# Block-sparse attention and a token mix on one core: V of a head pair kept in SBUF, value products in 32x32 tiles

## The chip, the cores and the metric

The kernel runs on one core of a Trainium2 chip. The metric is the device time of one execution in microseconds; before the change three runs took 635.79, 639.23 and 639.93 us, a median of 639.23. A profiled execution is a run of its own, and all rows of the profile below come from that one.

The engines are named as the profile names them: PE is the matrix engine (PEld its weight loads), DVE the vector engine, ACT the scalar engine, POOL the general-purpose engine and SP the engine that issues most of the DMAs.

## The reference

Attention over 4 batches, 8 heads, 768 tokens and a head size of 64, masked by blocks of 32 tokens. A query block sees its own and both neighbouring key blocks, the first and the last block, and three blocks that an input table names for it; the first and the last query block see everything. The result, heads side by side, goes through a token mix.

```python
scores = scale * np.matmul(q, k.transpose(0, 1, 3, 2))
mask = np.abs(blk_i - blk_j) <= window
mask = mask | (blk_i == 0) | (blk_j == 0) | (blk_i == n_blocks - 1) | (blk_j == n_blocks - 1)
for qb in range(n_blocks):
    for kb in sampled_blocks[qb]:
        mask[qb * block:(qb + 1) * block, kb * block:(kb + 1) * block] = True
attn = np.exp(scores)
attn = attn / (np.sum(attn, axis=-1, keepdims=True) + 1e-09)
...
theta = x @ w_theta
cos_t, sin_t = (np.cos(theta), np.sin(theta))
yr = np.einsum('ts,bsd->btd', w_tok_r, x * cos_t)
yi = np.einsum('ts,bsd->btd', w_tok_i, x * sin_t)
u = x + yr + yi
return u + np.maximum(u @ w_ch, 0.0)
```

The weights arrive as 64-bit floats. The kernel decodes them on the chip, piece by piece, into a high part of reduced precision and a low part that holds the rest; the token mix multiplies with both.

## The kernel before

A "pair" is two of the four batches, with all their heads: 16 heads, of which `b` numbers the batch (2), `e` a half of the heads (2) and `p` four heads of 32 columns each. The program does attention for both pairs and writes the result to a DRAM tile `xs`, then the token mix, which reads it back.

Attention works through 60 units. Of each pair, 8 are edge units (`"w"`: one batch, one half of the heads, the first or the last query block against all 24 key blocks) and 22 are inner units: one query block for all 16 heads against 8 key blocks. A unit passes through five stages: `scores` (PE, f32, tiles of 64 rows by 32 columns, so eight run side by side), a minimum over the negated scores (DVE), `weights` (ACT: exponentials), `turn` (PE: eight 128x128 transposes; ACT copies them out of PSUM) and `values` (PE: 128 rows, 32 columns, 65 moving columns of V and a column of ones), and `finish` (DVE divides by the sum; SP writes `xs`).

The eight key blocks of an inner unit stand in `kg`: ACT copies the neighbours and ends (line 235), DVE the three sampled blocks by numbers held in registers (line 244). Their values come straight from DRAM, row by row: the window blocks into `va` (line 263, a ring of three blocks, two tiles), the sampled blocks into `vb` by an indirect DMA from POOL (line 270, three tiles). The edge units' V comes in tiles `vw` of its own.

The order of the attention stage is written out by hand under `manual_schedule` (lines 403 to 445): in turn n, DVE finishes unit n-2, ACT and DVE gather keys for n+2, PE does the scores of n+1, the transposes of n and the values of n-1. So on PE the runs stand scores, transposes, values, in a steady round of 56 matmuls per inner unit as the program writes them. The decoding of the weights is spread over the turns in thirds of a piece (`Decoder.ahead` on ACT, `go` on DVE, 22 pieces). K of a pair lies in one tile `kb`; the second pair's K is loaded over it from the ACT queue when the first pair is nearly done.

The token mix has no hand-written order. Its matmuls run in f32r with high and low parts, 48 steps of theta (lines 517 to 519), mix (555 to 557) and an output product (578 to 580).

Of the kernel before, what the change touches and what calls it, by code (L numbers as in the profile page):

```python
# [10 lines left out]
F32 = mybir.dt.float32  # L11
# [8 lines left out]
P = 128  # L20
NB = 24
NP = 2
ZEROS = float(768 * NP)
VB_BUFS = 3
Q_AHEAD = 4
# [20 lines left out]
class Piece:  # L46
# [5 lines left out]
    def __init__(self, nc, hi, lo, src, name):  # L52
        self.nc, self.hi, self.lo, self.src, self.name = nc, hi, lo, src, name
        self.f = src.shape[1] // 2
# [10 lines left out]
    def bits(self):  # L65
        nc, a, ai = self.nc, self.a, self.a.bitcast(I32)
        nc.vector.tensor_scalar(a, a, WORD_LO, WORD_HI, op0=ALU.max, op1=ALU.min)
        nc.vector.tensor_scalar(ai, ai, 4, 1, op0=ALU.logical_shift_left, op1=ALU.logical_shift_right)
        nc.vector.scalar_tensor_tensor(ai, self.raw[:, :, 1], SIGN_BIT, ai, op0=ALU.bitwise_and, op1=ALU.bitwise_or)
# [12 lines left out]
    def low(self):  # L82
        self.nc.vector.tensor_tensor(self.a, self.a, self.hi.bitcast(F32), op=ALU.subtract)
        self.nc.vector.tensor_tensor(self.lo, self.a, self.raw[:, :, 0].bitcast(F32), op=ALU.add)


class Decoder:


    def __init__(self, pieces, pool, queue):  # L90
        self.pieces, self.pool, self.queue = pieces, pool, queue
        self.at = 0
        for piece in pieces[:2]:
            piece.load(pool, queue)

    def left(self):
        return max(3 * len(self.pieces) - self.at, 0)

    def ahead(self, n):

        for k in range(self.at, min(self.at + n, 3 * len(self.pieces))):
            piece = self.pieces[k // 3]
            if k % 3 == 0:
                piece.start()
            elif k % 3 == 2:
                piece.high()

    def go(self, n):
        for k in range(self.at, min(self.at + n, 3 * len(self.pieces))):
            piece = self.pieces[k // 3]  # L110
            (piece.bits, piece.rest, piece.low)[k % 3]()
            if k % 3 == 2 and k // 3 + 2 < len(self.pieces):
                self.pieces[k // 3 + 2].load(self.pool, self.queue)
        self.at += n


class Tables:


    def __init__(self, nc, cp, sampled):  # L120
        self.raw = cp.tile([P, NB * 6], I32, name="sb_raw")
        nc.sync.dma_start(self.raw, sampled.rearrange("i k -> (i k)").partition_broadcast(P))

    def make(self, nc, cp):
        raw = self.raw
        words = raw.rearrange("p (i k w) -> p i k w", k=3, w=2)
        given = cp.tile([P, 3, NB], F32, name="sb_given")
        nc.vector.tensor_copy(given, words[:, :, :, 0].rearrange("p i k -> p k i"))
        r = cp.tile([P, 3, NB], F32, name="sb_r")
        nc.vector.tensor_scalar(r, given, 0.0, float(NB - 1), op0=ALU.max, op1=ALU.min)  # L130
        self.block = cp.tile([1, NB * 3], I32, name="sb_block")
        nc.vector.tensor_copy(self.block.rearrange("p (i k) -> p k i", k=3), r[0:1])
        iota_i = cp.tile([P, NB], I32, name="iota_i")
        nc.gpsimd.iota(iota_i, pattern=[[1, NB]], base=0, channel_multiplier=0)
        qi = cp.tile([P, NB], F32, name="qi")
        nc.gpsimd.tensor_copy(qi, iota_i)
        first_i = cp.tile([96, NP], I32, name="first_i")
        for k in range(3):
            nc.gpsimd.iota(first_i[32 * k : 32 * k + 32], pattern=[[768, NP]], base=0, channel_multiplier=1)
        first = cp.tile([96, NP], F32, name="first_row")  # L140
        nc.gpsimd.tensor_copy(first, first_i)
# [3 lines left out]
        nc.vector.tensor_tensor(t, r, qi.unsqueeze(1).to_broadcast([P, 3, NB]), op=ALU.subtract)  # L145
# [9 lines left out]
        self.rows = rows = cp.tile([96, NP, NB], I32, name="rows")  # L155
        for k in range(3):
            g = slice(32 * k, 32 * k + 32)
            nc.vector.tensor_scalar(t[g, 0, :], u[g, k, :], -1.0, 1.0, op0=ALU.mult, op1=ALU.add)
            for bp in range(NP):
                nc.vector.tensor_scalar(t[g, 1 + bp, :], r[g, k, :], 32.0, first[g, bp : bp + 1], op0=ALU.mult, op1=ALU.add)  # L160
        left, base = t[0:96, 0:1, :], t[0:96, 1:3, :]
        nc.vector.scalar_tensor_tensor(base, base, -ZEROS, left.to_broadcast([96, NP, NB]), op0=ALU.add, op1=ALU.mult)
        nc.vector.tensor_scalar(rows, base, ZEROS, None, op0=ALU.add)


def attention(tc, qT, qE, kT, vr, sampled, xs, ident, pieces, follow):
# [9 lines left out]
    with ExitStack() as ctx, ExitStack() as early:  # L176
# [3 lines left out]
        ps_s = early.enter_context(tc.tile_pool(name="ps_s", bufs=2, space=PSUM, side="right"))  # L180
        gp = ctx.enter_context(tc.tile_pool(name="gp", bufs=1))
        vp = ctx.enter_context(tc.tile_pool(name="vp", bufs=2))
# [4 lines left out]
        ps_t = ctx.enter_context(tc.tile_pool(name="ps_t", bufs=1, space=PSUM))  # L187
        ps_x = ctx.enter_context(tc.tile_pool(name="ps_x", bufs=2, space=PSUM))
# [5 lines left out]
        kgs = [gp.tile([P, 8, 8, 32], F32, name=f"kg{x}") for x in range(2)]  # L194
        vas = [cp.tile([P, 1040], F32, name=f"va{x}") for x in range(2)]
        vbs = [cp.tile([P, 1040], F32, name=f"vb{x}") for x in range(VB_BUFS)]
        kbs, qbs, qes, vws, st, xws, numbers = {}, {}, {}, {}, {}, {}, {}
# [8 lines left out]
        def load_k(bp, b, p0=0, n=4, queue=nc.sync):  # L206
            if (b, p0) == (0, 0):
                kbs[bp] = kp.tile([P, 8, NB, 32], F32, tag="kb", name=f"kb{bp}")
            queue.dma_start(kbs[bp][:, 4 * b + p0 : 4 * b + p0 + n], kT[bp, b][:, p0 : p0 + n])

        def load_edges(bp):
            raw = ep.tile([P, 512], F32, tag="qw", name=f"qw{bp}")
            nc.sync.dma_start(raw, qE[bp])
            qes[bp] = raw

        def turn_edges(bp):
            t = ep.tile([P, 2, 2, 4, 32], F32, tag="qe", name=f"qe{bp}")
            nc.vector.tensor_scalar(t.rearrange("r z b p f -> r (z b p f)"), qes[bp], -0.125, None, op0=ALU.mult)
            qes[bp] = t
# [3 lines left out]
        def number_blocks(bp, i):  # L223
            _, numbers[bp, i] = nc.values_load_multi_w_load_instructions(
                tab.block[0:1, 3 * i : 3 * i + 3], engines=[mybir.EngineType.DVE], min_val=0, max_val=NB - 1,
                skip_runtime_bounds_check_because="Tables clamps the block numbers",
            )

        def gather_k(bp, i):
            kg, kb = kgs[i % 2], kbs[bp]  # L230
            def blocks(b0, n):
                return kb[:, :, b0 : b0 + n, :].rearrange("r g s f -> r s g f")

            def copy(s0, b0, n):
                nc.scalar.activation(kg[:, s0 : s0 + n], blocks(b0, n), AF.Copy, scale=-0.125)

            if i <= 2:
                copy(3, 0, 1)
                copy(7, NB - 1, 1)
            for b0, n in fresh(i, i <= 2):  # L240
                copy(b0 % 3, b0, n)
# [473 lines left out]
```

## Time and profile before

| | |
|---|---|
| Median of three runs | 639.23 us |
| The profiled execution | 636.82 us |
| Its span, first to last instruction | 635.0 us |
| Mean granted clock of PE | 0.964 |
| Busy in the span: PE, DVE, ACT, POOL | 563.2, 463.5, 361.0, 45.6 us |
| First matmul; first theta matmul | 8.45 us; 286.74 us |
| Moved by DMA | 96.52 MB, 152 GB/s over the span |

A group of instructions is shown with its line, engine and operation, what it writes and reads, the count, its busy time, the mean duration in ns, and after the second bar the idle time of the engine just ahead of it with what ended that. A wait is shown as who waited for whom, us in total, times, and the longest. "issue" as a releaser means that the engine waited for nothing that the profile shows. Busy time of PE is not PE at its peak, since matmuls overlap and their ends are modelled.

### The profile page before, as it was taken

The numbers are of one execution on the slowest core, as the hardware profiler recorded it, in microseconds if no ns is written. First come the engines' busy times: TensorE is split into PE (matmuls) and PEld (weight loads), VectorE is DVE, ScalarE is ACT, GpSimd is POOL, SyncE is SP. The second block draws the span as 40 slices with busy tenths as digits, with TensorE's granted clock in tenths as the row PEclk, the third lists the DMA queues.
The fourth block names the chain that finished last, engine by engine and source line by source line (L and its number), as shares of the span: only waits on it lengthen the run. The fifth ranks groups of instructions, "written<-read, shape, count | busy, mean of one in ns | idle before, by whom it ended". The sixth has DMA issues, their size and how long they took to land.

```text
span 635.0 us, 19148 instructions
## 1 busy us (share of the span) xinstructions
PE 563.2 (89%) x7808; PEld 483.1 (76%) x7808; DVE 463.5 (73%) x1239; ACT 361.0 (57%) x774; POOL 45.6 (7%) x56
## 2 busy tenths in 40 slices
PE   4987778769887768668999999999999999999997
PEld 1555545545455546547999999999999999999997
DVE  1897978875798878758999697575973767746554
ACT  1586768764587767656667564355642465524520
POOL 0101212211002211110000000000000000000000
PEclk9998989988898999887999999999999999999999
DMA  8859979999778997866542224211241211211002
GB/s 287 259 156 246 275 209 259 258 278 345 219 204 244 251 257 226 221 161 170 139 130 73 64 84 143 69 47 50 80 124 59 70 51 42 80 59 61 27 1 99
DMA packets 79959, 96.52 MB, mean 152 GB/s; under 512 B 5312, under 2 KB 64832, under 8 KB 79488
## 3 DMA queue, kind: packets, MB, share of 16 engines
q1 hardware_dynamic: 73088, 72.99, 39.2%
q0 software_dynamic: 4928, 17.57, 10.7%
q10 hardware_dynamic: 1856, 4.74, 2.1%
q8 instruction: 61, 1.00, 0.7%
q14 instruction: 26, 0.21, 0.1%
HBM read 82.70 MB, written 12.58 MB: 150 GB/s over the span
## 4 chain that ended last, share of the span: by engine, by line
PE 66%; DMA 18%; DVE 8%; issue 4%; ACT 2%; SPq 1%; DVEq 1%; ACTq 0%
PE y L555 10%; PE y L556 10%; PE y L557 10%; DMA va<-in_vr_dram 10%; PE X L318 4%; PE S L288 4%; PE T L307 4%; PE h L519 3%; PE h L518 3%; PE o L578 3%; PE h L517 3%; PE o L580 3%; PE o L579 3%; DMA kb<-in_kT_dram 3%; PE SW L357 2%
## 5 line engine op out<-in xcount | busy, mean ns | idle before, releaser
L300 ACT ACTIVATE P<-S,m 128x256 f32<-128x256 f32 x176 | 69.0, 477 | 15.1 <-DVE m L291 14.9
L307 PEld LDWEIGHTS T<-ident,P 128*128 128x128 f32 x352 | 42.1, 150 | 38.2 <-ACT P L300 25.9
L307 PE MATMUL T<-ident,P 128*128 128x128 f32 x352 | 60.5, 304 | 11.2 <-ACT P L300 6.1
L318 PE MATMUL X<-va,pT 128*32 128x65 f32 (+1 forms) x1408 | 50.3, 233 | 21.9 <-DMA va<-in_vr_dram 18.1
L291 DVE TENSOR_REDUCE m<-S 128x2 f32<-128x512 f32 x88 | 56.7, 686 | 16.7 <-PE S L288 9.8
L309 ACT COPY pT<-T 128x1024 f32<-128x1024 f32 x44 | 44.8, 1018 | 41.5 <-PE T L307 41.4
L288 PE MATMUL S<-kg,q 64*32 64x256 f32 x1408 | 55.1, 404 | 10.9 <-issue 10.9
L555 PE MATMUL y<-w_tok_r_hi,zh 128*128 128x384 f32 x192 | 64.6, 336 | 0.0
L556 PE MATMUL y<-w_tok_r_lo,zh 128*128 128x384 f32 x192 | 64.4, 335 | 0.0
L557 PE MATMUL y<-w_tok_r_hi,zl 128*128 128x384 f32 x192 | 64.3, 335 | 0.0
L556 PE MATMUL y<-w_tok_i_lo,zh 128*128 128x384 f32 x192 | 64.2, 334 | 0.0
L555 PE MATMUL y<-w_tok_i_hi,zh 128*128 128x384 f32 x192 | 64.2, 334 | 0.0
L557 PE MATMUL y<-w_tok_i_hi,zl 128*128 128x384 f32 x192 | 62.7, 334 | 0.0
L270 POOL DMA_INDIRECT vb<-in_vr_dram,rows x44 | 44.1, 1002 | 229.3 <-PE X L318 206.0
L318 PEld LDWEIGHTS X<-va,pT 128*32 128x32 f32 (+1 forms) x1408 | 35.6, 116 | 31.8 <-DMA va<-in_vr_dram 17.8
L517 PE MATMUL h<-w_theta_hi,xTh 128*128 128x256 f32 x192 | 55.8, 290 | 1.9 <-ACT xTh L508 1.9
L519 PE MATMUL h<-w_theta_hi,xTl 128*128 128x256 f32 x192 | 55.6, 290 | 0.5 <-DVE xTl L509 0.5
L518 PE MATMUL h<-w_theta_lo,xTh 128*128 128x256 f32 x192 | 55.3, 288 | 0.0
L318 PE MATMUL X<-vb,pT 128*32 128x65 f32 (+1 forms) x1408 | 49.8, 232 | 5.0 <-issue 5.0
L521 ACT ACTIVATE t<-h,up_int 128x256 f32<-128x256 f32 x48 | 22.7, 473 | 42.7 <-PE h L519 42.0
L528 ACT ACTIVATE cs<-rr 128x256 f32<-128x256 f32 x48 | 20.0, 416 | 45.8 <-DVE rr L526 45.8
L578 PE MATMUL o<-uh,w_ch_hi 128*128 128x384 f32 x128 | 42.5, 336 | 0.9 <-DVE of L584 0.9
(125 smaller groups left out, 1337.2 us busy)
## 6 DMA issues: line engine op xcount, KB each, us to landing
xa<-xs SPq DMA_DIRECT2D x192, 64.0 KB
va<-in_vr_dram SPq DMA_DIRECT2D x30, 260.0 KB
xr<-xs SPq DMA_DIRECT2D x24, 256.0 KB
out_dram<-of SPq DMA_DIRECT2D x32, 192.0 KB
q<-in_qT_dram SPq DMA_DIRECT2D x22, 256.0 KB
xs<-xo SPq DMA_DIRECT2D x44, 128.0 KB
vw<-in_vr_dram SPq DMA_DIRECT2D x6, 780.0 KB
raw_tok_r<-in_w_tok_r_dram SPq DMA_DIRECT2D x9, 512.0 KB
```

The lines of the kernel that those rows point to most:

```text
L288: nc.tensor.matmul(sc[32 * p : 32 * p + 32, e, b, :], q[rows, b, p, :], kg[rows, :, 4 * b + p, :], start=True, stop=True)
L291: nc.vector.tensor_reduce(m[:, e], sc[:, e], axis=AX.X, op=ALU.min)
L300: nc.scalar.activation(pt[:, e, b, :], sc[:, e, b, :], AF.Exp, bias=m[:, e, b : b + 1], scale=-1.0)
L307: nc.tensor.transpose(t[:, k, :], pt, ident)
L318: nc.tensor.matmul(x[32 * p : 32 * p + 32, g, :], pt[0:rows, k, 32 * p : 32 * p + 32], v[0:rows, v0 + 65 * p : v0 + 65 * p + 65], start=st ...
L517: nc.tensor.matmul(ps, hi[:, c, :], wh[:, c, :], start=c == 0, stop=False)
L518: nc.tensor.matmul(ps, hi[:, c, :], wl[:, c, :], start=False, stop=False)
L519: nc.tensor.matmul(ps, lo[:, c, :], wh[:, c, :], start=False, stop=c == 3)
L555: nc.tensor.matmul(acc, zh[:, dd], wh[:, j, tt], start=j == 0 and m == 0, stop=False)
L556: nc.tensor.matmul(acc, zh[:, dd], wl[:, j, tt], start=False, stop=False)
L557: nc.tensor.matmul(acc, zl[:, dd], wh[:, j, tt], start=False, stop=j == 5 and m == 1)
L578: nc.tensor.matmul(ps, wh[:, c, :], uh, start=c == 0, stop=False)
```

## The change

K and V of a pair lie in SBUF whole. There are two places, `kv0` for the first pair (it later takes the token weights' second part) and tiles of their own for the second. V is laid out by groups of 32 rows, (batch, half of the heads) to a group of partitions and a key block to 260 columns, and loaded in six pieces of 8 blocks, K and V in turn, on SP's queue.

Inner units read the three neighbouring blocks where they lie. The sampled blocks are copied on the chip: two key blocks by DVE and one by ACT into `kg` (now five blocks), three value blocks by POOL into `vg`, each engine with block numbers in registers of its own. A block that is masked or doubled is replaced by a block of zeros in V.

The value product is cut by row group: for each of eight key blocks, 4 x 2 matmuls of 32 rows, 32 columns and 65 moving columns for each batch `b`. The two batches go in two runs, with the scores and transposes of other units between them, and the second run waits for the first reduction of those scores. `X` covers two banks and has one buffer; the transposes' PSUM tile is split into two of one bank.

Edge units are cut by key blocks, not by heads: (z, t), z the first or last query block and t a third of the key blocks, six of a pair, each with all heads and 8 blocks, the same shape as an inner unit. Each third has its own maximum; POOL scales the three sums by the exponentials of the differences and adds them.

Decoding of weights: 20 pieces, theta and half of tok_r with the first pair, the rest with the second; DVE does two parts of a piece, the low part goes to POOL in two halves. w_ch is decoded in eight steps of the token mix, a whole piece each. The scale by 0.125 moves from the copies into the exponential.

Cut to its core:

```diff
-        ps_t = ctx.enter_context(tc.tile_pool(name="ps_t", bufs=1, space=PSUM))
-        ps_x = ctx.enter_context(tc.tile_pool(name="ps_x", bufs=2, space=PSUM))
+        ps_t = ctx.enter_context(tc.tile_pool(name="ps_t", bufs=2, space=PSUM))
+        ps_x = ctx.enter_context(tc.tile_pool(name="ps_x", bufs=1, space=PSUM))
...
-            for k, number in enumerate(numbers.pop((bp, i))):
-                src = kb[:, :, bass.ds(number, 1), :].rearrange("r g s f -> r s g f")
-                nc.vector.tensor_scalar(kg[:, 4 + k : 5 + k], src, -0.125, None, op0=ALU.mult)
...
-                nc.sync.dma_start(va[s0 : s0 + 32 * n], vr[768 * bp + 32 * b0 : 768 * bp + 32 * (b0 + n)])
...
-            nc.gpsimd.indirect_dma_start(
-                out=vb[0:96],
...
+            for k in range(2):
+                nc.vector.tensor_copy(kg[:, 1 + k : 2 + k], block(bp, numbers[bp, i][0][k]))
...
+            nc.scalar.copy(kg[:, 3:4], block(bp, numbers[bp, i][0][2]))
...
+            for k in range(3):
+                nc.gpsimd.tensor_copy(vg[:, k : k + 1], vs[bp][:, bass.ds(numbers[bp, i][1][k], 1)])
...
+                q, runs = qes[bp][:, z], [(0, ks[bp][:, 8 * t : 8 * t + 8])]
+            else:
+                q, runs = qbs.pop((bp, i)), [(0, ks[bp][:, i - 1 : i + 2]), (3, kgs[i % 2])]
...
-            for p in range(4):
-                nc.tensor.matmul(
-                    x[32 * p : 32 * p + 32, g, :], pt[0:rows, k, 32 * p : 32 * p + 32], v[0:rows, v0 + 65 * p : v0 + 65 * p + 65],
-                    start=start, stop=stop,
-                )
...
+            for k in used:
                 for p in range(4):
                     for e in range(2):
+                        rows = slice(32 * (2 * b + e), 32 * (2 * b + e) + 32)
+                        mm = nc.tensor.matmul(
+                            s["X"][32 * p : 32 * p + 32, e, 65 * b : 65 * b + 65], s["T"][rows, k, 32 * p : 32 * p + 32],
+                            blocks[k][rows, 65 * p : 65 * p + 65], start=k == used[0], stop=k == used[-1],
+                        )
...
+                do(n - 1, values, 0)
+                do(n + 1, scores)
+                between = st[units[n + 1]]["reduced"] if n + 1 < len(units) else None
+                do(n, turn)
...
+                do(n - 1, values, 1, between)
+                do(n, evict)
+                do(n + 1, weights)
+                do(n - 1, finish)
```

The order on PE, inner units of the first pair, before: the scores of unit 4, the transposes of 3, the values of 2. `S`, `T`, `X` are the PSUM tiles of the three stages with the unit's number, `pT` the transposed weights; a row ends with the shape and the count.

```order
L288 MATMUL S_4_842<-kg_116,q_3_141 32x256 x16
L307 MATMUL T_3_862<-ident,P_3_778 128x128 x8
L318 MATMUL X_2_882<-va_118,pT_2_776 32x65 x4
L318 MATMUL X_2_882<-vb_122,pT_2_776 32x65 x4
L318 MATMUL X_2_882<-va_118,pT_2_776 32x65 x4
L318 MATMUL X_2_882<-vb_122,pT_2_776 32x65 x4
L318 MATMUL X_2_882<-va_118,pT_2_776 32x65 x4
L318 MATMUL X_2_882<-vb_122,pT_2_776 32x65 x4
L318 MATMUL X_2_882<-va_118,pT_2_776 32x65 x4
L318 MATMUL X_2_882<-vb_122,pT_2_776 32x65 x4
```

One round is 56 matmuls. The same place on PE after the change, where `kv` is the first pair's place and `vg` the copied blocks:

```order
L284 MATMUL S_4_1691<-kv_122,q_3_769 32x96 x8
L284 MATMUL S_4_1691<-kg_113,q_3_769 32x160 x8
L284 MATMUL S_4_1691<-kv_122,q_3_769 32x96 x8
L284 MATMUL S_4_1691<-kg_113,q_3_769 32x160 x8
L326 MATMUL T_3_0_1729<-ident,P_3_1579 128x128 x4
L326 MATMUL T_3_1_1730<-ident,P_3_1579 128x128 x4
L355 MATMUL X_2_1626<-kv_122,pT_2_1576 32x65 x32
L355 MATMUL X_2_1626<-vg_115,pT_2_1576 32x65 x24
L355 MATMUL X_2_1626<-kv_122,pT_2_1576 32x65 x8
L355 MATMUL X_3_1843<-kv_122,pT_3_1803 32x65 x32
L355 MATMUL X_3_1843<-vg_116,pT_3_1803 32x65 x24
L355 MATMUL X_3_1843<-kv_122,pT_3_1803 32x65 x8
```

A round is 168 matmuls now, and the last half of one unit's values stands right ahead of the first half of the next unit's, which writes the same `X`. An edge unit on PE before (`SW`, `Tw` and `XW` are its tiles):

```order
L357 MATMUL SW_011_271<-kb_131,qe_129 32x512 x4
L357 MATMUL SW_011_271<-kb_131,qe_129 32x256 x4
L307 MATMUL Tw_010_282<-ident,PW_010_242 128x128 x6
L318 MATMUL XW_0_244<-vw_0_0_134,pTw_001_240 32x65 x24
L357 MATMUL SW_100_323<-kb_131,qe_129 32x512 x4
```

and after:

```order
L284 MATMUL S_w_273<-kv_122,qe_120 32x256 x16
L326 MATMUL T_w_0_294<-ident,P_w_201 128x128 x4
L326 MATMUL T_w_1_295<-ident,P_w_201 128x128 x4
L355 MATMUL X_w_208<-kv_122,pT_w_198 32x65 x64
L355 MATMUL X_w_406<-kv_122,pT_w_368 32x65 x64
```

There were 38 matmuls to an edge unit and 16 such units; there are 152 to one and 12 units.

On DVE, inner units, before: the division of unit 4 and after it the three copies of sampled keys.

```order
L325 TENSOR_SCALAR sm_4_1104<-X_4_1069 128x4
L326 RECIPROCAL sm_4_1104<-sm_4_1104 128x4
L328 TENSOR_TENSOR xo_4_1107<-X_4_1069,sm_4_1104 128x256
L244 ISA
L244 TENSOR_SCALAR kg_116<-kb_131 128x256
```

and after, the reduction of unit 4, the division of unit 2 and two copies:

```order
L295 TENSOR_REDUCE m_4_1724<-S_4_1691 128x2 x2
L298 TENSOR_SCALAR nm_4_1727<-m_4_1724 128x4
L368 TENSOR_SCALAR sm_2_1811<-X_2_1626 128x4
L369 RECIPROCAL sm_2_1811<-sm_2_1811 128x4
L371 TENSOR_TENSOR xo_2_1814<-X_2_1626,sm_2_1811 128x256
L234 TENSOR_LOAD sb_keys
```

The division now stands right behind the reduction of the scores two units on; it is what frees `X`.

More of the change, by code (lines that the diff above doesn't have):

```diff
@@ L602, in token_mix @@
         stage = late.enter_context(tc.tile_pool(name="stage2", bufs=1))
[L603 removed]
+        ch = ch_pieces()
+        for piece in ch[:2]:
+            piece.load(stage, nc.sync)
         for k in range(2, RAW_AHEAD):
@@ L664, in sparse_attention_then_token_mix, with first_place, second, tok @@
-    early = pieces("theta", 512) + [x for pair in zip(pieces("tok_r", 512), pieces("tok_i", 512)) for x in pair]
-    attention(tc, qT, qE, kT, vr, sampled.bitcast(I32), xs, ident, early, follow)
+    def first_place(shape, dtype, name):
+        return const.tile(shape, dtype, tag="place", name=name)
+    rest = []
+    def second():
+        if not rest:
+            rest.append(first_place([P, 2, 9 * 768], F32R, "w_second"))
+        return rest[0]
+    def tok(at):
+        tile_, k = (first, at) if at < 3 else (second(), at - 3)
+        return [tile_[:, x, 768 * k : 768 * k + 768] for x in range(2)]
```

532 lines of the change are left out of this document (273 added, 259 removed).

## The prediction

> **What bounds the kernel now.** I read the table by stage first, then the groups of instructions, then the waits, and last the timeline at the places where TensorE waits for nothing that a semaphore shows. The stage table (time, each engine's busy time and count, granted clock, DMA share, GB/s) cuts the execution at the first matmul and at the first theta matmul of the token mix:
>
> ```profile
> core 0: us, PE busy (x) PEld busy (x) DVE busy (x) ACT busy (x) POOL busy (x), PEclk, DMA share, GB/s
> 8.44:286.74 278.30, 221.84 (x5632) 143.48 (x5632) 217.51 (x559) 188.24 (x363) 44.09 (x44) 0.94 0.86 243
> 286.74:635.00 348.26, 341.38 (x2180) 339.64 (x2176) 245.42 (x675) 171.23 (x410) 0.00 (x0) 0.99 0.26 78
> ```
>
> Attention takes 278.3 us with the DMA engines at 0.86 and no compute engine full; the token mix takes 348.3 us with PE full. So attention is where the change can act, and its obvious limits are the transfers of V. The groups and waits say more:
>
> ```profile
> q8 instruction: 61, 1.00, 0.7%
> ...
> L318 PE MATMUL X<-va,pT 128*32 128x65 f32 (+1 forms) x1408 | 50.3, 233 | 21.9 <-DMA va<-in_vr_dram 18.1
> L288 PE MATMUL S<-kg,q 64*32 64x256 f32 x1408 | 55.1, 404 | 10.9 <-issue 10.9
> ...
> PE X L318 <- DMA va<-in_vr_dram: 18.1, 14, 3.5
> PEld SW L357 <- issue: 25.2, 40, 8.4
> PEld X L318 <- issue: 18.3, 42, 2.3
> PEld S L288 <- issue: 16.0, 18, 4.5
> PE S L288 <- issue: 10.9, 5, 4.0
> ```
>
> TensorE waits for "issue" about as long as for the tile `va`. What that is: the page counts 7808 matmuls and 7808 weight loads, 15,616 instructions, and queue q8 carried 61 packets and 1.00 MB: 16 KB each, so 256 instructions of TensorE in each packet. Call that a page of code. The timeline shows stops in the middle of a run of equal matmuls, where no semaphore can be at fault:
>
> ```profile
> 88.05 1.09 PE L288 MATMUL S<-kg,q 64*32 64x256 f32 x11 [3.75 <-issue]
> 98.98 0.26 PE L318 MATMUL X<-vb,pT 128*32 128x65 f32 x3 [0.59 <-issue]
> 103.62 0.26 PE L318 MATMUL X<-va,pT 128*32 128x65 f32 x4 [0.97 <-issue]
> 237.66 1.08 PE L288 MATMUL S<-kg,q 64*32 64x256 f32 x8 [4.02 <-issue]
> ```
>
> Cut at such stops, every stretch holds one page (127 matmuls, 127 loads, a wait or two):
>
> ```profile
> 98.98:103.62 4.64, 3.67 (x127) 2.77 (x127) 4.27 (x13) 4.06 (x9) 1.09 (x1) 1.00 0.76 233
> 103.62:109.33 5.71, 4.16 (x127) 2.71 (x126) 5.29 (x16) 4.43 (x11) 1.96 (x2) 1.00 1.06 285
> 109.33:115.14 5.81, 4.15 (x126) 2.73 (x127) 4.50 (x14) 4.57 (x10) 1.22 (x2) 1.00 1.03 274
> 115.14:121.96 6.82, 5.39 (x127) 3.52 (x126) 5.78 (x15) 4.44 (x9) 1.26 (x1) 1.00 0.99 278
> 121.96:125.90 3.94, 3.72 (x126) 2.76 (x127) 3.18 (x10) 3.08 (x8) 0.91 (x1) 1.00 0.80 204
> 125.90:130.10 4.20, 3.72 (x127) 2.76 (x127) 3.88 (x12) 3.80 (x8) 1.21 (x1) 1.00 0.78 203
> 225.59:229.16 3.57, 3.56 (x126) 2.68 (x127) 2.70 (x9) 2.45 (x5) 0.91 (x1) 1.00 0.74 185
> ```
>
> Six pages in a row ended in a stop, 3.94 to 6.82 us each (mean 5.2); the last row is a page without a stop behind it. The stop of 3.75 us at 88.05 fits one late packet, which the DMA view of 85.30 to 86.60 us holds:
>
> ```profile
> q8 instruction: 1, 0.02, 5.7%
> ```
>
> 5.7% of 16 engines over 1.30 us is 1.19 us of transfer; TensorE went on at 88.05, some 1.5 us after the window. I read from this that TensorE holds the page it runs and one ahead, that the next is asked for when a page is entered, and that asking, transfer and arrival take 3.6 us or more, longer the busier the DMA engines. Before, that is nearly hidden: a unit issues 208 instructions.
>
> **The change part by part.** Value matmuls: 32 per inner unit become 128 (32 rows each, 65 columns), scores 16 become 32 (96 and 160 columns), eight transposes stay. The profile counts each value and score matmul twice (L288: 1408 records, 16 issued in each of 44 units) and each record has its weight load. Inner unit before: (32+8+64) x 2 = 208 instructions; after (64+8+256) x 2 = 656, and 592 in the four units with seven blocks. Edge units: 16 of (16+6+48) x 2 = 140 before; 12 of (32+8+256) x 2 = 592 after. Attention in all: 44 x 208 + 16 x 140 = 11,392, or 44.5 pages, against 40 x 656 + 16 x 592 = 35,712, or 139.5 pages.
>
> Price of a page. Above, 3.57 us without a stop bounds it from above at a DMA share of 0.74; with stops, 3.94, 4.20 and 4.64 us at 0.76 to 0.80, and 5.71 to 6.82 at 0.99 to 1.06. After the change attention moves about 39 MB (K and V once 12.7, q 6.3, xs 6.3, weights 11.5, code 2.3); over some 550 us that is 71 GB/s, as in the token mix now (78 GB/s, share 0.26). Lower end 3.4 us: 3.57 less a little for a packet that isn't held up. Upper end 4.6. I take 3.9, in the middle of 3.57, 3.94 and 4.20.
>
> A page takes longer to come than to run: it holds one half of a unit's values (about 1.05 us, below) or scores, transposes and a few values (about 2.5 us). So a step of 656 instructions takes 656/256 x 3.9 = 10.0 us, and what else the change does lies inside it. `X` has one buffer now, so the values of a unit wait for the division of the one before: about 1.0 us, inside. The transfers of V by row, the indirect gathers and the edge tiles go: attention moves 39 MB where it moved 67.6 (243 GB/s over 278.3 us), and the waits on `va` go with them; late next is the code. Key copies (DVE two, ACT one), value copies and the weights' low parts on POOL, a second copy out of PSUM on ACT: DVE and ACT had 217.5 and 188.2 us in 60 units, 3.6 and 3.1 per unit, so some 4 of 10 us. The merged edge maxima: under 2 us on POOL, twice per pair. All of these cost nothing as long as the step is 10 us; without that cover they are the first rival. Decoding w_ch in eight steps rather than twelve: the same work on DVE, taken as 0, with 3 us either way.
>
> Start: the first third of K with the edge queries is 1.3 MB, the first matmul stays at 8.4 us; 3 us until the pages that lie ready are used up (139.5 less 1.5). In the first 30 us 7.6 MB of K, V and weights are in flight: eight pages at 5.2 instead of 3.9, 10 us more. Sum: 8.4 + 3 + 138 x 3.9 (538) + 10 + 348.3 + 1.8 outside the span (636.82 against 635.0) = 910 us. The runs' median, 639.23, is 0.4% over the profiled 636.82; I leave that out.
>
> The rule that speaks against this sum: the Trainium skill, Runtime: NRT & Kernel Launch, Instruction fetch mechanics, gives TensorE room for 2048 instructions and calls the fetch hidden, and a sentence later says two lines of 16 KiB, read in order. By the first, three steps of code would lie ready and the sum would be the first rival's; by the second it is mine. The stops at every 256 instructions above agree with two lines.
>
> **The rivals.**
>
> *The code comes in time.* Then TensorE and the single `X` set the step. Rows for it, a score run, a transpose run, a value run and the division's three instructions:
>
> ```profile
> 99.68 1.09 PE L288 MATMUL S<-kg,q 64*32 64x256 f32 x32
> 100.70 1.09 PE L307 MATMUL T<-ident,P 128*128 128x128 f32 x8
> 101.73 0.32 PE L318 MATMUL X<-va,pT 128*32 128x65 f32 x8
> ...
> 228.11 0.32 PE L318 MATMUL X<-va,pT 128*32 128x65 f32 x8
> 229.15 1.09 PE L288 MATMUL S<-kg,q 64*32 64x256 f32 x32
> ...
> L325 DVE TENSOR_SCALAR sm<-X 128x4 f32<-128x4 f32 x44 | 6.8, 156 | 12.7 <-PE X L318 12.4
> L326 DVE RECIPROCAL sm<-sm 128x4 f32<-128x4 f32 x44 | 7.8, 178 | 1.4
> L328 DVE TENSOR_TENSOR xo<-X,sm 128x256 f32<-128x256 f32 x44 | 18.7, 424 | 3.0 <-DMA xs<-xo 1.6
> ```
>
> Scores 1.02, transposes 1.03, 64 value records on four tiles 1.04 us. After, the two halves run apart, 128 records on eight tiles each: 1.04 twice if the tiles fill. With 0.76 us of division and its semaphores (1.0), a step is 5.2 us: 8.4 + 56 x 5.2 + 348.3 + 1.8 = 650 us. If no record starts sooner than now (1.04/64 = 16 ns), values take 4.2, the step 7.2, the time 762. For it: the token mix never stops for code. Against it: seven rows above. The Trainium skill, TensorE: Matmul & The Clock Gate, puts the floor between starts at about 25 ns; the trace's 16 ns lies under it, so it gets no chance of its own; by 25 ns the estimate would be 8.4 + 56 x 9.5 + 350 = 890.
>
> *Faster.* The same, with the division hidden and 4.1 us a step: 8.4 + 56 x 4.1 + 350 = 588 us. It decides where a step falls under (637 - 358.5)/56 = 5.0 us, a page under 1.9 us; the trace has none under 3.5.
>
> *The clock falls as well.* After an idle stretch TensorE runs at half speed:
>
> ```profile
> 282.50 2.42 PE L307 MATMUL T<-ident,P 128*128 128x128 f32 x8 [4.78 <-ACT P L300]
> ```
>
> 2.42 us for what took 1.09. Idle stretches would be under 3 us here, against 4.78, so I don't expect it; if it held throughout, the page with scores and transposes would run 4.9 us: 56 more, 966 us. Pages as slow as before (5.2) give 1090.
>
> **How the numbers follow.** Forecast (pages at 3.4 to 4.6 us) 0.78; slow clock or slow pages 0.10; code in time 0.08; faster 0.04. Predicted 910 us. Range: 138 x 3.4 + 372 = 840 to 138 x 4.55 + 372 = 1000, which leaves out the two rivals with code in time and the worst of the slow pages, 2 in 10. About 1% is what a measurement here can tell from no change: faster 0.04, within 1% 0.03 (the first rival's low edge), slower 0.93.
>
> **What would show it.** Right: q8 with about 176 packets (45,184 instructions) where it had 61; stretches of 256 instructions with a stop behind each, near 3.9 us; "issue" at the head of TensorE's waits with some 300 us; a DMA share near 0.25 in attention; token mix near 348 us. Wrong: steps of 5 to 7 us with waits on DVE before X, or several pages fetched at once. The step most at risk is the price of a page when the DMA engines are quiet, which no stretch of attention now shows.

## The result, and the profile after

The changed kernel takes 958.1 us (median of four runs, 950.9 to 959.59) where the kernel before takes 639.42 in the same comparison: a ratio of 1.498, 95% interval 1.490 to 1.506. The profiled execution is the run of 950.9 us, with a span of 949.1 us and a mean granted clock of 0.744 (0.964 before). One run of those below is left out, the second of the kernel with half the value matmuls and two buffers for X (783.3 us): it lies over 1.5% above the other run of its kernel.

The stage table of the changed kernel, with the columns of the prediction's first fence, cut at 8.44 us as before and at 600.60 us, a microsecond short of the end of attention's matmuls (the first matmul starts at 6.40 us now, and the first 24 theta matmuls run between the last values, from 580.50 us on):

```profile
8.44:600.60 592.16, 446.82 (x17783) 348.37 (x17769) 227.23 (x569) 192.60 (x438) 135.12 (x232) 0.60 0.20 65
600.60:948.50 347.90, 337.94 (x2156) 336.75 (x2155) 239.71 (x655) 164.78 (x396) 0.00 (x0) 0.98 0.25 75
```

The token mix is where it was: 347.9 us. All the loss lies in attention, 592.2 us for 278.3. The transfers did go: the DMA share there fell from 0.86 to 0.20. DVE, ACT and POOL are busy for 227, 193 and 135 of the 592 us. PE is busy for 447, and its clock is 0.60 of full speed. The page shows the clock in 40 slices, the instruction queue and the chain:

```profile
PEclk7655565655666675555755565699999999999999
...
q8 instruction: 156, 2.56, 1.1%
...
PE 72%; issue 12%; DVE 7%; DMA 4%; ACT 4%; SPq 0%; POOL 0%; POOLq 0%; ACTq 0%; DVEq 0%
```

156 packets of code where there were 61. The clock drops as attention starts and returns when it ends. PE's waits, matmuls first and weight loads behind them, show no DMA of V any more; "issue" and the single `X` stand in its place:

```profile
PE X L355 <- DVE xo L371: 34.8, 32, 3.1
PE X L355 <- issue: 34.0, 41, 2.1
PE S L284 <- issue: 29.0, 21, 2.3
PE X_w L355 <- issue: 16.9, 13, 3.0
...
PEld X L355 <- issue: 54.4, 60, 3.3
PEld S L284 <- issue: 42.3, 63, 2.9
PEld T L326 <- issue: 28.9, 47, 3.2
```

No stop of PE in these rows is longer than 3.3 us. The timeline shows again stops inside runs of equal matmuls (the bracket is the idle time ahead of a row):

```profile
487.58 0.57 PE L355 MATMUL X<-vg,pT 32*32 32x65 f32 x23 [0.25 <-issue]
...
493.25 0.71 PE L355 MATMUL X<-v,pT 32*32 32x65 f32 x50 [1.19 <-issue]
...
496.96 1.09 PE L355 MATMUL X<-v,pT 32*32 32x65 f32 x53 [0.84 <-issue]
...
500.63 0.38 PE L284 MATMUL S<-k,q 64*32 64x96 f32 x4 [1.22 <-issue]
...
502.49 1.97 PE L326 MATMUL T<-ident,P 128*128 128x128 f32 x8
```

The table of the stretches between those stops, columns as above:

```profile
487.58:493.25 5.67, 4.47 (x127) 3.39 (x128) 2.63 (x5) 2.46 (x6) 0.00 (x0) 0.69 0.47 153
493.25:496.96 3.71, 1.85 (x129) 1.47 (x128) 1.86 (x7) 1.68 (x5) 1.21 (x4) 0.68 0.12 40
496.96:500.63 3.67, 2.45 (x128) 1.94 (x129) 0.53 (x1) 0.00 (x0) 1.98 (x2) 0.50 0.02 4
```

Each holds one page of 256 instructions. With the DMA engines at 0.02 it takes 3.67 us, of which PE is busy for 2.45; at 0.12, 3.71 with PE busy for half. The page of 5.67 us ran while a 256 KB transfer of q went by: its code came late. The trace ties the stops to the packets: of the 65 stops on "issue" of over 0.5 us in attention, nine in ten end 1.2 to 1.6 us after the latest packet of q8 landed, while the packets come some 4 us apart. That the transposes of 502.49 took 1.97 us where 1.09 is the full-clock time shows the third thing, the lowered clock.

### The profile page after: what moved, and what is told of

Read it like the earlier page. It is cut to its first block, busy times and chain, and to the rows that moved or that the text cites. A ratio compares the mean times of both kernels' runs of the same rounds, so it can differ in the third digit from the quotient of the medians.

```text
span 949.1 us, 43861 instructions
## 1 busy us (share of the span) xinstructions
PE 786.8 (83%) x19968; PEld 686.4 (72%) x19968; DVE 467.1 (49%) x1229; ACT 358.9 (38%) x836; POOL 136.6 (14%) x242
## 4 chain that ended last, share of the span: by engine, by line
PE 72%; issue 12%; DVE 7%; DMA 4%; ACT 4%; SPq 0%; POOL 0%; POOLq 0%; ACTq 0%; DVEq 0%
PE X L355 16%; PE S L284 10%; PE T L326 8%; PE y L579 6%; PE y L581 6%; PE y L580 6%; PE X_w L355 5%; PE S_w L284 3%; PE T_w L326 2%; PE o L602 2%; PE o L603 2%; PE o L604 2%; PE h L543 2%; PE h L542 2%; PE h L541 2%
## 5 line engine op out<-in xcount | busy, mean ns | idle before, releaser
L355 PE MATMUL X<-v,pT 32*32 32x65 f32 x3456 | 74.0, 279 | 35.3 <-DVE xo L371 15.4
L355 PE MATMUL X<-kv,pT 32*32 32x65 f32 x3456 | 72.0, 274 | 37.3 <-DVE xo L371 19.5
L579 PE MATMUL y<-w_second,zh 128*128 128x384 f32 x288 | 97.3, 338 | 2.4 <-ACT zh L566 2.4
L580 PE MATMUL y<-w_second,zh 128*128 128x384 f32 x288 | 97.3, 338 | 0.0
L581 PE MATMUL y<-w_second,zl 128*128 128x384 f32 x288 | 93.3, 338 | 0.0
L355 PE MATMUL X<-vg,pT 32*32 32x65 f32 x4224 | 85.2, 280 | 8.5 <-issue 7.6
L284 PE MATMUL S<-kg,q 64*32 64x160 f32 x1408 | 77.4, 470 | 14.2 <-issue 14.2
L355 PEld LDWEIGHTS X<-vg,pT 32*32 32x32 f32 x4224 | 66.4, 127 | 11.6 <-issue 10.5
L314 ACT ACTIVATE P<-S,nm 128x256 f32<-128x256 f32 x176 | 69.2, 484 | 0.0
L579 PEld LDWEIGHTS y<-w_second,zh 128*128 128x128 f32 x288 | 54.8, 190 | 2.6 <-ACT zh L566 2.6
L580 PEld LDWEIGHTS y<-w_second,zh 128*128 128x128 f32 x288 | 54.9, 191 | 0.0
L581 PEld LDWEIGHTS y<-w_second,zl 128*128 128x128 f32 x288 | 54.5, 191 | 0.0
```

The source lines that it names most:

```text
L284: nc.tensor.matmul(sc[32 * p : 32 * p + 32, e, b, 32 * s0 : 32 * (s0 + n)], q[rows, b, p, :], keys[rows, :, 4 * b + p, :], start=True, sto ...
L314: nc.scalar.activation(pt[:, :, 2 * b + e], sc[:, e, b].rearrange("r (s f) -> r s f", s=8), AF.Exp, bias=nm[:, 2 * e + b : 2 * e + b + 1], ...
L355: mm = nc.tensor.matmul(s["X"][32 * p : 32 * p + 32, e, 65 * b : 65 * b + 65], s["T"][rows, k, 32 * p : 32 * p + 32], blocks[k][rows, 65 * ...
L579: nc.tensor.matmul(acc, zh[:, dd], wh[:, tt], start=j == 0 and m == 0, stop=False)
L580: nc.tensor.matmul(acc, zh[:, dd], wl[:, tt], start=False, stop=False)
L581: nc.tensor.matmul(acc, zl[:, dd], wh[:, tt], start=False, stop=j == 5 and m == 1)
```

## The experiments

Three theories. A: PE waits for its code, and a page costs some 3.6 to 4.2 us whatever it holds. B: array time, at the lowered clock and with the single `X`, sets the step, and code comes beside it. C: the clock, and what lowers it. The text calls the changed kernel "after". Times are medians, of two runs for those of one round and of four for those of three rounds, against 958.1 for after and the kernel before's own median of the same comparison (635.5 to 641.5).

### A page of code more, before and after

Each of the 44 inner units gets 64 matmuls of one column ahead of its scores, into the place that the scores overwrite. In the kernel before:

```diff
             sc = ps_s.tile([P, 2, 2, 256], F32, tag="S", name=f"S{bp}_{i}")
+            for _ in range(8):
+                for p in range(4):
+                    for e in range(2):
+                        rows = slice(64 * e, 64 * e + 64)
+                        nc.tensor.matmul(sc[32 * p : 32 * p + 32, e, 0, 0:1], q[rows, 0, p, :], kg[rows, 0, 0, 0:1], start=True, stop=True)
```

> The kernel before, with 64 matmuls of one column (256 TensorE instructions, one page of code) added to each of the 44 inner units; their results are overwritten by the scores. Theory A (TensorE waits for the arrival of its code): a unit goes from 208 to 464 instructions, 0.81 to 1.81 pages; at 3.9 to 5.2 us a page that is 7.1 to 9.4 us where a unit now takes 4.8, so +100 to +205 us, 740 to 845. Theory B (array time sets the step, code is hidden): 128 records of one column at no more than 16 ns are 1.0 to 2.0 us a unit, partly beside other waits: +0 to +88 us, 640 to 728. Theory C on the clock: if stops for code are what lowers the granted clock, attention falls from 0.94 to under 0.8 here, with matmuls of 128 rows as before; if it is the 32-row value tiles, it stays over 0.9.

Measured: 811.5 us, +169.9 over the 641.5 beside it (ratio 1.266, 1.256 to 1.275), or 3.86 us for each added page, with what the lowered clock below adds.

The same in the changed kernel, with K's own tile in `kg`'s place.

> The changed kernel with the same 64 matmuls of one column (one page of code) in each of the 44 inner units. Theory A (code): 44 pages more at 3.6 to 4.2 us, +158 to +185 us, 1115 to 1145. Theory B (array time at the lowered clock, with X's single buffer and DVE): 128 records of one column, at most 2 us at half clock and partly in waits, +0 to +88 us, 958 to 1046.

Measured: 1121.3 us, +163.2, or 3.71 us a page (ratio to before 1.749, 1.729 to 1.768). Both lie in A's range and far outside B's. The groups of this kernel show what the added matmuls did, busy time and mean duration, and behind the second bar the idle time ahead of them:

```profile
L283 PE MATMUL S<-kv,q 64*32 64x1 f32 x2816 | 34.3, 195 | 55.7 <-issue 55.7
L283 PE MATMUL S<-k,q 64*32 64x1 f32 x2816 | 34.2, 195 | 52.3 <-issue 52.3
```

68.5 us of array time in 44 units, and 108.0 us of waiting for nothing but "issue". The kernel before, whose value tiles have 128 rows, lost its clock with the added page. Its stage table with the page and without it:

```profile
20.00:459.00 439.00, 338.84 (x11282) 245.56 (x11274) 222.08 (x564) 187.62 (x365) 40.72 (x44) 0.75 0.54 150
...
20.00:286.74 266.74, 210.29 (x5578) 139.81 (x5577) 212.66 (x541) 185.74 (x360) 44.09 (x44) 0.93 0.85 237
```

Stops for code came in, and so did matmuls that use little of the array; which of them lowers the clock, this run doesn't tell.

### Fewer score matmuls over the same columns

ACT copies the three window blocks into `kg` too, and the scores become 16 matmuls of 256 columns again.

```diff
+            nc.scalar.copy(kg[:, 0:3], ks[bp][:, i - 1 : i + 2].rearrange("r s g f -> r s (g f)"))
...
-                q, runs = qbs.pop((bp, i)), [(0, ks[bp][:, i - 1 : i + 2]), (3, kgs[i % 2])]
+                q, runs = qbs.pop((bp, i)), [(0, kgs[i % 2])]
```

> The changed kernel with the three window blocks of K copied into the key tile by ScalarE, so that a unit's scores are 16 matmuls of 256 columns where they were 32 of 96 and 160: the same columns, 64 instructions less in each of 44 inner units; the weights' tile has one buffer, to make room. Theory A (code): 2816 instructions are 11 pages less, at 3.6 to 4.2 us: -40 to -46 us, 910 to 920. Theory B (array time): the columns are the same, so 0, or a few us more for ScalarE's copy: 955 to 975.

Measured: 911.7 us, -46.4, or 4.2 us for each of 11 pages (ratio to before 1.422, 1.413 to 1.431). The columns are the same, and ACT does more than before. A again, though the clock rose a little as well (0.65 in attention for 0.60), and its part in the 46 us isn't known.

### The same in the other direction, in the kernel before

Only the split of the scores into 96 and 160 columns is taken over from the change.

```diff
-                        nc.tensor.matmul(sc[32 * p : 32 * p + 32, e, b, :], q[rows, b, p, :], kg[rows, :, 4 * b + p, :], start=True, stop=True)
+                        for s0, s1 in ((0, 3), (3, 8)):
+                            nc.tensor.matmul(
+                                sc[32 * p : 32 * p + 32, e, b, 32 * s0 : 32 * s1], q[rows, b, p, :], kg[rows, s0:s1, 4 * b + p, :], start=True, stop=True
+                            )
```

> The kernel before with its scores in 32 matmuls of 96 and 160 columns for 16 of 256, as the change has them, and nothing else of it: 64 instructions more in each of 44 inner units, 11 pages, the same columns. Theory A0 (the kernel before stands already at the pace of its code, so each page more costs what it did with a page more per unit, 3.9 us): +43 us, about 682. Theory B0 (272 instructions, 1.06 pages at 3.6 to 4.2 us, still fit under the 4.8 us of a unit): 0 to +12 us, 639 to 651.

Measured: 666.1 us, +30.6 over 635.5 (ratio 1.047, 1.039 to 1.055), or 2.8 us a page: between the two, nearer to A0. The waits of its matmuls have "issue" ahead of the scores at their head, with 26.4 us where it was 10.9:

```profile
PE S L289 <- issue: 26.4, 17, 5.2
PE X L321 <- DMA va<-in_vr_dram: 15.7, 7, 3.5
```

So the kernel before stands close to the edge: of the 3.7 us that a page costs, three quarters are felt at once. This part of the change alone is a tenth of its loss (30.6 of 319).

### More traffic

Two transfers of 393 KB in each unit from the seventh on, to a tile that nobody reads.

```diff
+                if 6 <= n:
+                    for s0 in (0, 3):
+                        nc.sync.dma_start(more, kT[0][:, s0 : s0 + 3])
```

> The changed kernel with two more transfers of 393 KB in each unit from the seventh on, into a tile that nothing reads: some 70 GB/s more, DMA share 0.18 to about 0.4 in attention. Theory A (a page costs what asking and transfer take, longer the busier the DMA engines): between 4.2 us a page at 0.18 and 5.1 at 0.52 in the kernel before with a page more, so about 4.7: +50 to +90 us, 1005 to 1050. Theory B (array time at the lowered clock): the added transfers are used by nobody, 0 to +10 us.

Measured: 980.0 us, +21.9 (ratio to before 1.530, 1.518 to 1.543), with the DMA share doubled to 0.40:

```profile
20.00:625.00 605.00, 434.64 (x17450) 339.61 (x17447) 223.71 (x562) 187.82 (x427) 135.47 (x232) 0.61 0.40 120
```

Neither: traffic that no one reads does cost, as it would if code had to get past it, but 0.16 us a page (21.9 over 139.5) rather than the 0.5 that A had worked out. That expectation rested on 5.1 us a page in the kernel before with its added page, which is attention's whole time there divided by its pages, the waits on V among them. What one added page costs in that kernel was 3.86.

### Two buffers for X

`S` gives up one of its two buffers for a second `X`.

```diff
-        ps_s = early.enter_context(tc.tile_pool(name="ps_s", bufs=2, space=PSUM, side="right"))
+        ps_s = early.enter_context(tc.tile_pool(name="ps_s", bufs=1, space=PSUM, side="right"))
+        ps_x = early.enter_context(tc.tile_pool(name="ps_x", bufs=2, space=PSUM, side="right"))
...
-        ps_x = ctx.enter_context(tc.tile_pool(name="ps_x", bufs=1, space=PSUM))
```

> The changed kernel with two buffers for X and, to make room, one for S. The values of a unit no longer wait for the division of the one before (34.8 us in 32 waits). Theory A (code): the waits lie in pages whose code isn't there yet, or is asked for later by as much: -20 to 0 us, 938 to 958. Theory B (TensorE's own chain of X, array and DVE sets the step): -35 to -60 us, 898 to 923.

Measured: 946.7 us, -11.4 (ratio to before 1.478, 1.466 to 1.490, which just touches after's 1.490 to 1.506): A's range, and outside B's. The wait on the division (34.8 us) is gone from the list, and "issue" ahead of the same matmuls has grown from 34.0 to 79.1:

```profile
PE X L355 <- issue: 79.1, 50, 2.8
PE S L284 <- issue: 38.5, 21, 3.4
```

The wait taken away is given to the next in line, the code.

### Half the value matmuls

Two heads in one matmul: 64 matmuls a unit in place of 128.

```diff
-                for p in range(4):
+                for p in range(0, 4, 2):
...
-                            s["X"][32 * p : 32 * p + 32, e, 65 * b : 65 * b + 65], s["T"][rows, k, 32 * p : 32 * p + 32],
-                            blocks[k][rows, 65 * p : 65 * p + 65], start=k == used[0], stop=k == used[-1],
+                            s["X"][32 * p : 32 * p + 64, e, 130 * b : 130 * b + 130], s["T"][rows, k, 32 * p : 32 * p + 64],
+                            blocks[k][rows, 65 * p : 65 * p + 130], start=k == used[0], stop=k == used[-1],
```

> The changed kernel with the value products of two heads in one matmul (64 rows of output, 130 columns): 64 matmuls a unit for 128, the same columns in all, but half as many tiles of the array beside each other. The odd heads' own products fall in columns that are not read, so the odd heads' output is left out. Attention goes from 35,712 TensorE instructions to 21,504, from 139.5 pages to 84. Theory A (code): 84 pages at 3.6 to 4.2 us, 672 to 723 us. Theory B (array time sets the step): values take twice as long, 0.9 us a half becomes 1.8 at full clock and 3.6 at half: a step of 6.8 us, 740, if the clock comes back with the stops gone, and of 11.6 us, 1010, if it stays at half.

Measured: 895.4 us, -62.7 (ratio to before 1.398, 1.386 to 1.411). Neither number. The code had nearly stopped binding: in the list of matmul waits "issue" is down to a microsecond or so in each row. What held it then was the wait for `X`, and the clock:

```profile
PE X L355 <- DVE xo L371: 40.6, 38, 1.6
...
PE X L355 <- issue: 1.2, 1, 1.2
```

The timeline has whole steps at both clocks. Rows of the scores, the values behind the wait for `X` and the transposes, from two steps in a stretch of full clock and then from two where it fell:

```profile
161.25 0.40 PE L284 MATMUL S<-kv,q 64*32 64x96 f32 x16
...
166.46 1.12 PE L355 MATMUL X<-kv,pT 32*64 32x130 f32 x32 [1.05 <-DVE xo L371]
...
168.40 0.40 PE L284 MATMUL S<-kv,q 64*32 64x96 f32 x16
...
169.54 1.09 PE L326 MATMUL T<-ident,P 128*128 128x128 f32 x8
...
185.05 0.57 PE L284 MATMUL S<-kv,q 64*32 64x96 f32 x16
...
192.49 1.25 PE L355 MATMUL X<-kv,pT 32*64 32x130 f32 x32 [1.06 <-DVE xo L371]
...
195.40 0.57 PE L284 MATMUL S<-kv,q 64*32 64x96 f32 x16
...
197.29 1.97 PE L326 MATMUL T<-ident,P 128*128 128x128 f32 x8
```

A step takes 168.40 - 161.25 = 7.15 us, or 195.40 - 185.05 = 10.35 us, with the same instructions and the same wait of a microsecond for `X`. Between the two stretches lie one stop for code and one wait for `X`, close together:

```profile
180.91 0.27 PE L355 MATMUL X<-kv,pT 32*64 32x130 f32 x1 [1.21 <-issue]
182.20 1.19 PE L355 MATMUL X<-kv,pT 32*64 32x130 f32 x32 [1.02 <-DVE xo L371]
```

### Half the value matmuls, and two buffers for X

The two edits above together. If short stops lower the clock, it should come back here.

> The pairs of heads (odd heads' output left out, as there) with two buffers for X and one for S besides: almost no stop for code is left and no wait for the division. With the pairs alone a step took 7.15 us in stretches of full clock and 10.2 us in stretches where the clock fell. Theory C2 (the granted clock falls because TensorE stops, however shortly: for code, for X): the clock is over 0.9 in attention and a step takes 1.93 + 1.93 + 2.05 = 5.9 us, or the 1.56 pages that it needs at 3.6 to 4.2 us, 5.6 to 6.6: 690 to 735 us. Theory C3 (the clock falls because tiles of 32 rows use a part of the array only): the clock stays near 0.7, the step at 8 to 9 us: 810 to 870.

Measured: 771.5 us, one run, some 120 us less than with the pairs alone (895.4). The stage tables, of both kernels in this order, then the new one's waits:

```profile
20.00:420.00 400.00, 360.48 (x10606) 305.95 (x10606) 225.38 (x570) 182.03 (x421) 135.66 (x232) 0.88 0.27 84
...
20.00:540.00 520.00, 461.45 (x10536) 385.92 (x10539) 225.20 (x562) 187.24 (x427) 135.34 (x232) 0.73 0.20 62
```

```profile
PE X L355 <- issue: 10.8, 10, 2.5
PE S L284 <- DVE kg L256: 10.7, 15, 1.3
```

The clock is 0.88 with tiles that are still 32 rows high, where it was 0.73 with a wait of a microsecond in most steps. So tiles of 32 rows alone don't hold the clock down, as C3 has it, and the waits count, as C2 has it. But C2 is not the whole of it: the clock isn't over 0.9, a step with the wait of 1.05 us can keep full clock, as the rows of the pairs show, and the last section finds that the kind of matmuls goes with it as well. C2's time doesn't hold either: 771.5 lies 36 us above its range. Some stops for code are left, with stretches of low clock behind them, and scores now wait for DVE's key copies. Which of these holds how much of the 36 us stays open.

The same second buffer brought 11 us in the changed kernel and some 120 us here. In the one case the code was next in line, in the other it hardly was.

### Wide matmuls, to keep the clock up

Two matmuls of 128 rows and 512 columns more in each unit, ahead of the scores.

```diff
+            for _ in range(2):
+                nc.tensor.matmul(sc[:, 0].rearrange("r b f -> r (b f)"), ident, ks[bp][:, 0:2].rearrange("r s g f -> r (s g f)"), start=True, stop=True)
```

> The changed kernel with two matmuls of 128 rows and 512 columns more per unit (8 TensorE instructions; 1.7 us of array time at full clock, 3.4 us at half), overwritten by the scores. Theory A (code alone, the low clock costs little): 448 instructions are 1.75 pages, +7 us, and the array time lies in the stops for code: 950 to 985. Theory C1 (the clock is low because the array is too little used, and the low clock costs time): the granted clock returns to over 0.9 in attention and pages run at the pace of the code, 3.5 us: 870 to 930. Theory B (array time at the low clock sets the step): +56 times 3.4 us, about 1150, clock as low as before.

Measured: 1048.2 us, +90.1 (ratio to before 1.635, 1.626 to 1.644). Inconclusive as a test of what the clock costs. The clock did rise, to 0.78 in attention, not to 0.9; but the added matmuls themselves took long, 3.45 us a unit on average and 3.78 at the low clock, as in this row:

```profile
302.70 3.78 PE L279 MATMUL S<-kv,ident 128*128 128x512 f32 x4
```

Over 56 units that is 193 us of array time for 90 us more: about half of it found room in the stops. What the lowered clock alone costs the changed kernel was not separated.

### Fewer matmuls in the kernel before

Value products of two heads in one matmul for three of four (batch, head half) groups, in 130 columns; the fourth group doesn't fit the bank.

```diff
-            for p in range(4):
+            w = 2 if g < 3 else 1
+            for p in range(0, 4, w):
                 nc.tensor.matmul(
-                    x[32 * p : 32 * p + 32, g, :], pt[0:rows, k, 32 * p : 32 * p + 32], v[0:rows, v0 + 65 * p : v0 + 65 * p + 65],
-                    start=start, stop=stop,
+                    x[32 * p : 32 * p + 32 * w, 130 * g : 130 * g + 65 * w], pt[0:rows, k, 32 * p : 32 * p + 32 * w],
+                    v[0:rows, v0 + 65 * p : v0 + 65 * p + 65 * w], start=start, stop=stop,
                 )
```

> The kernel before with the value products of two heads in one matmul in three of four (batch, head half) groups: 20 matmuls for 32 in an inner unit. What is read and written out are the first columns of X, so the attention output is left out of its right place in part. Attention goes from 11,392 TensorE instructions to 8,704, from 44.5 pages to 34; the array's time for values rises by some 0.8 us a unit. Theory A (the kernel before is held by code as well): 10.5 pages less, at 3.6 to 5.2 us, less what the waits on V's tiles take back: -20 to -50 us, 590 to 620. Theory B (transfers of V or array time set its step, code does not): 0 to +35 us, 640 to 675.

Measured: 658.3 us, +19.1 over 639.2 (ratio 1.029, 1.022 to 1.035): B's range, and theory A misses. The list of its matmul waits names what came instead. "issue" is gone from its head, and the wait on the rows of V, 18.1 us before, is 32.3:

```profile
PE X L319 <- DMA va<-in_vr_dram: 32.3, 15, 4.9
```

The waits on V and the longer values on the array, not separated here, take back more than 10.5 pages of code save. So in the kernel before these three stand close together, and taking from one at the cost of another lost.

## Why the prediction was right

The median of 958.1 us lies in the range of 840 to 1000 and 48 us over the 910, the profiled run 41 us over it.

*What bounds it.* Right. The forecast was one page of code after another, 139.5 of them; a page more cost 3.71 us (the added page, after), with 64 columns more in a unit; eleven fewer saved 4.2 each (the 16 scores), with the same columns; the traffic of data stayed the same in both.

*The price of a page.* The step that was mis-sized: taken as 3.9 us, between 3.4 and 4.6. By the sum's own terms, attention ended at 600.6, so that the 138 pages took (600.6 - 8.4 - 3)/138 = 4.27 us with the term for the crowded start in it; forecast were (538 + 10)/138 = 3.97. That 0.3 us a page is 41 us, the difference between 910 and the profiled 950.9: the other terms, 348.3 for the token mix and 1.8 outside the span, came out at 348.5 and 1.8. (Cut where the prediction cuts, at the first theta matmul, some 134 pages ahead of 580.50 us took 4.24 us each.) The trace shows where it lies, in the 138 intervals between packets of q8 in attention, 4.21 us on average. In 71 of them the other queues' DMA share is under 0.05: they last 3.87 us, the shortest 3.30, so that 3.9 was right for quiet engines. In 23 it is 0.4 or more: they last 5.23 us, at the same granted clock (0.58 and 0.59). So the mean lies higher with the pages that meet a transfer, which the prediction had allowed for at the start alone. The single `X` holds 11 us of the 41; what the low clock adds to a page isn't separated.

*The rule about room for 2048 instructions.* The sum kept to two lines of code, and the runs agree with it. The Trainium skill, Runtime: NRT & Kernel Launch, Instruction fetch mechanics, also says that the fetch is hidden because dispatch is the slower of the two. Here the measurement decides against it. A dispatch that takes 3.71 us for 256 instructions would need 14 ns for each; but behind the stop at 143.91 us (last fence below) 80 one-column matmuls with their loads, 160 instructions, start within 0.78 us, 5 ns each. So the added page costs 3.71 us because it arrives late; its array time is 1.56 us (68.5 us in 44 units).

*What lies inside a step.* Right. DVE, ACT and POOL have hundreds of microseconds to spare, and `X`'s single buffer, put down as inside, was worth 11 us. It was inside only because the code was late: with half the value matmuls it and the clock behind it were worth some 120.

*The transfers that go.* Right that they bring nothing: DMA share 0.20 and 65 GB/s, where 71 GB/s and a share near 0.25 were forecast, and what was late next is the code.

*"The clock falls as well".* The rival with 966 us happened, beside the forecast rather than in place of it. The argument against it, that idle stretches would be under 3 us where the trace had 4.78, failed: they are 3.3 at most and the clock was 0.60 all through attention. The Trainium skill, TensorE: Matmul & The Clock Gate, HAM oscillation, names idle gaps over about 3.4 us as what brings the clock down; by that rule too it should have stayed up. The traces show that shorter stops add up (last section). That the number held without a term for the clock is in part luck. A page that waits for code has room in it for matmuls at half speed (2.45 of 3.67 us busy above), so the low clock was paid for only in part; how much of the 41 us is its, no run separates.

*The rivals with code in time.* They didn't happen, since the code didn't come in time. What a step of this layout takes with its code in time, no run shows. The nearest is half the value matmuls, whose values take twice as long on the array: 7.15 us a step at full clock, with the wait for `X`.

*The tell-tales.* Stretches of one page with a stop behind, the DMA share and the token mix are as told. Two were wrong. "About 176 packets" does not follow from its own counts: 35,712 instructions in attention and the 15,616 - 11,392 = 4,224 of the rest are 39,936, or 156 packets, which is what queue q8 carried; the sum used 139.5 and isn't touched. And "some 300 us" of issue was too much: the rows shown above have 80 us for matmuls and 126 for weight loads, partly the same time, since at the low clock PE was busy for 447 of 592 us.

## What to carry to other kernels

Count TensorE's instructions as a cost of their own: in this kernel 256 of them cost 3.7 us if nothing else in the stretch takes that long, so a stage has a floor of instructions/256 times 3.7 us, and cutting a product into four times as many matmuls, each four times smaller, multiplies that floor. Before saving transfers, ask what stands next: here a quarter of a page more in each unit was felt already. And try two small repairs together where a third limit hides both: the second buffer was worth 11 us behind the code and some 120 without it.

None of these kernels beats the one before. In this layout even the pairs, at full clock and without a stop, take 5.4 us a step (1.09 for scores, 1.09 for transposes and 3.41 for values, less their overlap), which an estimate from these rows puts at 8.4 + 56 x 5.4 + 350 = 661 us.

## What the hardware showed beside that

```profile
215.78 3.41 PE L355 MATMUL X_w<-v,pT_w 32*64 32x130 f32 x128
219.12 1.09 PE L284 MATMUL S_w<-k,qe 64*32 64x256 f32 x32
220.14 1.09 PE L326 MATMUL T_w<-ident,P_w 128*128 128x128 f32 x8
221.17 2.29 PE L355 MATMUL X_w<-v,pT_w 32*64 32x130 f32 x87
```

These rows are of the last estimate, from the timeline of the pairs with two `X`: 221.17 - 215.78 = 5.39 us for a step. Three things were not expected:

- The granted clock falls without a long stop. With no stop over 3.3 us it was 0.60 over 592 us. In the clock records of these traces it changes between full and half only, and every 3.41 us or a multiple of that. In the kernel before, all 9 such stretches of attention at full clock in which PE sat idle for 2.06 us or more were followed by half clock, and none of the 58 with 1.82 us or less was. In the changed kernel 33 of 34 were, with an idle time from 0.71 us on; with the pairs 31 of the 35 that were had 1.04 us or more. In these three it went back to full only behind stretches with at most 0.6 us idle, and not behind each. So idle time adds up over 3.41 us, and the kernels with small value tiles bear less of it; why is not shown.
- Code waits behind other transfers: a page took 3.67 us at a DMA share of 0.02 and 5.67 us while 256 KB of q were moving; over all of attention 3.87 us at a share under 0.05 and 5.23 at 0.4 or more.
- Matmuls of one column start every 10 ns, as a run in the kernel before with its added page shows, 80 records in 144.69 - 143.91 = 0.78 us:

```profile
143.91 0.90 PE L288 MATMUL S<-kg,q 64*32 64x1 f32 x80 [0.56 <-issue]
144.69 1.10 PE L293 MATMUL S<-kg,q 64*32 64x256 f32 x32
```
